# Heads 9, 17 and 25 by key layout in float32, their tiles one to two among those of the next two heads

## The chip, the cores and the metric

The kernel runs on one core of a Trainium2 chip. The metric is the device time of one execution in microseconds (us); several runs are given by their median. A profile of one execution shows what each engine did: PE (TensorE, matrix products), DVE (VectorE), ACT (ScalarE), POOL (GpSimd), SP (SyncE, which here issues most DMAs), and the 16 DMA engines.

## The reference

LSH attention on four batches of 8 heads, 768 positions, 64 wide, and then an MLP with spatial gating on the joined heads of each batch. Cut to what matters:

```
mask   = bucket(q) == bucket(k)                 # 6 hash bits, signs of q@proj, k@proj
scores = where(mask, q @ k.T / 8, -1e9)         # (4, 8, 768, 768)
scores = scores - max(scores, -1)
attn   = exp(scores) / (sum(exp(scores), -1) + 1e-9)
x      = (attn @ v) -> (4, 768, 512)
h      = relu(x @ w_in);  u, g = h[..., :512], h[..., 512:]
g      = (g - mean(g)) / sqrt(var(g) + 1e-6)
g      = einsum('ts,bsd->btd', w_spatial, g) + b_spatial
out    = (u * g) @ w_out
```

## The kernel before

Heads are numbered 0 to 31 (8 to a batch), pairs 0 to 15. A head has six **tiles** of 128 rows. A loop over g counts tiles: before, tile i of head n is worked on at g = 6n + i. In each step the loop names scores, value products, the preparation of later heads, the conversion of MLP weights and MLP units, and gives every piece a priority by `at(g + offset, k)`. A scheduler then puts the instructions of each engine in order by these priorities and by when it reckons them ready; each engine runs its list strictly in order, and so does each DMA queue.

**Query layout** (`scores`, head not in `KEYS`): the tile has 128 queries on the partitions and 768 keys along the row. Four fp16 matmuls (L291, L292; the hash mask is part of the product) fill a PSUM tile `sp`; DVE takes the row minimum of the scaled scores (L293, `jk`, result `nb`); ACT the exponential with that bias (L295, `ex`); ACT casts it to the fp16 high part (L298) and DVE or POOL subtracts to get the low part (L299), both into `pp`; a DMA transpose (L301) brings `pp` to `pt` with the keys on the partitions. Five tiles later (`LAG`) `weighted` multiplies `pt` with the fp16 high and low parts of v (`vp`): 18 matmuls (L314 to L316).

**Key layout** (`KEYS` = heads 1 to 7): the tile has 128 keys on the partitions. The row maximum must be known before: `row_max` makes the scores in query layout once more (two matmuls, L241), DVE takes their maximum (L243), and after the sixth tile the maxima are transposed on PE (L251) and sent by a small DMA into row 127 of the operand `ab` (L254). `scores_k` then needs four matmuls (L262, L263) and one exponential (L265, float32, into the same ring `pt` of `PTB` = 5 tiles); there is no cast, no subtraction and no transpose. Three tiles later (`LAGK`) `weighted_k` multiplies in float32 with `vf`, the values of a pair in float32 (L275). The row maxima of head n are named from `NT + LEAD` = 10 tiles before its first tile.

**Preparation.** `load_qk`, `hash_rows`, `split_qk` work by pairs; `build(n)` at g = 6(n - 2) issues the DMAs that fill one of four operands `ab` (L199 to L212): hash rows (`ab<-sg`, from ACT's queue for heads 8 and up) and the halves of q and k (`ab<-hl`, from SP's). `split_v` and `mean_v` prepare the values. `normalize` divides a finished head by its sum, `transpose_x` turns a pair for the MLP by DMA (`xt`).

**MLP.** When the last head of a batch is normalized, its 28 units (`vps`, `ups`, `sps`, `ops`) join a queue; a credit of 28/48 a step takes one out every 1.7 steps, so that the MLP of a batch runs on PE among the heads of the next one. That of batch 3 runs alone at the end.

PSUM has two tiles for scores (`sc`), two for value products (`pv`), two for the rest.

Of the kernel before, what the change touches and what calls it, by code (L numbers as in the profile page):

```python
# [19 lines left out]
P = 128  # L20
# [16 lines left out]
def lsh_attention_spatial_gating(  # L37
# [116 lines left out]
    def load_v(p):  # L154
        b, r = divmod(p, NPAIR)
        if has_queries(p):
            v32 = st["v32", p] = ld.tile([P, 2 * NT, D], F32, tag="v32", bufs=1, name=f"v32_{p}")
            LQ.dma_start(out=v32, in_=v[b, r])

    def load_vf(p):  # L160
        b, r = divmod(p, NPAIR)
        if has_keys(p):
            LQ.dma_start(out=vf[p % 2][:, :, 0:D], in_=v[b, r])

    def has_keys(p):
        return 2 * p in KEYS or 2 * p + 1 in KEYS

    def has_queries(p):
        return not (2 * p in KEYS and 2 * p + 1 in KEYS)

# [22 lines left out]
    def build(n):  # L193
        p, e = divmod(n, 2)
        hl, sg, t = st["hl", p], st["sg", p], ab[n % NAB]
        r = slice(D * e, D * e + D)
        q_s, q_h = (BQ_S[n >= NH], BQ_H[n >= NH])
        if n < 1:
            nc.sync.dma_start(out=t[0:D, 2:4], in_=hl[r, 1:3])  # L199
        for j in range(4):  # L200
            q_s.dma_start(
                out=t[D:NR, 3 - j // 2, (j % 2) * HS:(j % 2 + 1) * HS],
                in_=sg[32 * j + 16 * e:32 * j + 16 * e + 2 * NB, :])
        if n < 1:
            q_h.dma_start(out=t[0:D, 0:2], in_=hl[r, 0:2])
# [15 lines left out]
    def mean_v(p):  # L221
# [6 lines left out]
        nc.gpsimd.tensor_add(c, c, a[:, 4:6])  # L228
        mp = ps_m.tile([P, 512], F32, tag=MT, name=f"mp{p}")
        nc.tensor.matmul(mp[:, :P], lhsT=ones, rhs=c.rearrange("p e d -> p (e d)"), start=True, stop=True)  # L230
        fm = wk.tile([P, 2, D], F32, tag="fm", bufs=2, name=f"fm{p}")
        nc.scalar.activation(fm.rearrange("p e d -> p (e d)"), mp[:, :P], AF.Copy, scale=SX / S)
        st["fm", p] = fm

    def row_max(n, i):
        t = ab[n % NAB]
        if i == 0:
# [6 lines left out]
        if i == NT - 1:  # L244
            nb = st["nb", n] = wk.tile([P, NT], F32, tag="nb", bufs=3, name=f"nb{n}")
            mx = st.pop(("mx", n))
# [9 lines left out]
    def scores_k(n, i):  # L256
        t = ab[n % NAB]
        ps = ps_sc.tile([P, 2, 512], F32, tag="sc", name=f"sp{n}_{i}")[:, :, :HS]
# [9 lines left out]
    def weighted_k(n, i):  # L268
# [5 lines left out]
        for qi in range(NT):  # L274
            nc.tensor.matmul(acc[:, qi, :], lhsT=ex[:, qi * P:(qi + 1) * P], rhs=vf[p % 2][:, 2 * i + e, :],  # L275
                             start=(i == 0 and qi == 0), stop=(i == NT - 1 and qi == NT - 1))

    def scores(n, i):
        if n in KEYS:
            scores_k(n, i)  # L280
            return
        t = ab[n % NAB]
        if i == 0:
            st["nb", n] = wk.tile([P, NT], F32, tag="nb", bufs=3, name=f"nb{n}")
        nb = st["nb", n][:, i:i + 1]
# [32 lines left out]
    def normalize(n):  # L318
# [14 lines left out]
        nc.gpsimd.tensor_add(x, x, f)  # L333
        if e == 0:
            st["xs", p] = wk.tile([P, 2, NT, P], F16, tag="xs", bufs=2, name=f"xs{p}")
# [114 lines left out]
    PL_POOL = (2,)  # L450
    KEYS = {1, 2, 3, 4, 5, 6, 7}
    PL_POOL1 = (0,3)
# [32 lines left out]
    def at(g, k):  # L485
        tc.cur_priority = int(1000 * (g + 40) + k)

    at(-40, 0)
    nc.sync.dma_start(out=hc, in_=hconst)
# [11 lines left out]
    credit = 0.0  # L501
    wv = 0
    rml = [(NT * n + i - NT - LEAD, n, i) for n in sorted(KEYS) for i in range(NT)]
    for g in range(N * NT + LAG):
        n, i = divmod(g, NT)
        if n < N:
            at(g + G_S, 0)
            scores(n, i)
            r = n // 2
# [10 lines left out]
            while rml and rml[0][0] <= g:  # L520
                row_max(*rml.pop(0)[1:])
            at(g + G_P, 300)
            stack = ExitStack()
            if n not in KEYS:
                stack.enter_context(tc.issue_after(st["tr"]))
            if BQ_S[n + 2 >= NH] is nc.scalar or BQ_H[n + 2 >= NH] is nc.scalar:
                stack.enter_context(tc.issue_after(st["ex", n, i]))
            if i == BI and n + 2 < N:
                build(n + 2)
            if n % 2 == 0:  # L530
# [16 lines left out]
            stack.close()  # L547
        while wv < N * NT and wv + (LAGK if wv // NT in KEYS else LAG) <= g:
            m, j = divmod(wv, NT)
            wv += 1  # L550
            at(g + G_V, 200)
            weighted(m, j)
            if j == NT - 1:
                at(g + G_N, 250)
                normalize(m)
                if m % 2:
                    transpose_x(m // 2)
                    if m % NH == NH - 1:
                        queue += mlp_units(m // NH)
        at(g + G_W, 500)  # L560
# [53 lines left out]
```

## Time and profile before

| | |
|---|---|
| median of 3 runs | 738.57 us (736.13 to 741.49) |
| profiled execution, first to last instruction (span) | 741.7 us |
| mean granted PE clock | 0.937 |
| busy: PE, DVE, ACT, POOL | 631.5, 520.6, 434.8, 321.2 us |
| DMA | 120.95 MB, mean 163 GB/s |

The profile gives the span of the profiled execution, 0.4% above the median; no other time of that execution is shown. A row of a group is: line, engine, operation, output <- inputs, shape, count | busy us, mean ns of one | idle time of the engine before them and what ended it. A row of the timeline or of the chain begins with its start and its length in us; a row of waits gives the total, the number and the longest. Matmuls are pipelined, so a matmul's own duration is longer than the distance to the next one; distances are what count for PE.

### The profile page before, as it was taken

The page shows a single profiled execution, that of the slowest core. Times are in us where ns is not written, and L with a number is a line of the kernel's source. Part 1 is how long each engine was busy: PE and PEld are TensorE (multiplying, and loading weights), DVE is VectorE, ACT ScalarE, POOL GpSimd, SP SyncE. Part 2 cuts the span into 40 slices and gives each one's busy share as a digit, 9 for nine tenths or more (in the row PEclk, how much of TensorE's full clock was granted, in tenths as well). Part 3 has the DMA queues.
Part 4 walks back from the last instruction along what each step waited for, and adds up shares of the span by engine and source line. Part 5 has one row for each costly group of instructions (what it writes and reads, how often), then busy time and mean ns, then how long its engine had stood idle before and what let it go on. Part 6 is the DMA issues. An engine that isn't in the chain of part 4 may idle for free.

```text
span 741.7 us, 14927 instructions
## 1 busy us (share of the span) xinstructions
PE 631.5 (85%) x5759; PEld 400.4 (54%) x5759; DVE 520.6 (70%) x945; ACT 434.8 (59%) x668; POOL 321.2 (43%) x324
## 2 busy tenths in 40 slices
PE   1569898998988776997898899889898998999997
PEld 0237686776445444554544555556455565654553
DVE  4677795536799999567689798678698987755200
ACT  1344574346788676655676577667677776743221
POOL 5122443123458675264314565156235571451503
PEclk9768797999999989898999999999999999999999
DMA  9565554324999989996999799999999999860011
GB/s 235 149 123 155 133 148 102 99 55 97 224 237 197 215 207 187 213 178 138 234 202 199 138 210 213 211 211 212 206 210 181 194 175 213 182 136 15 1 42 43
DMA packets 290011, 120.95 MB, mean 163 GB/s; under 512 B 270740, under 2 KB 273812, under 8 KB 289940
## 3 DMA queue, kind: packets, MB, share of 16 engines
q1 hardware_dynamic: 287636, 119.11, 76.4%
q10 hardware_dynamic: 2304, 0.89, 0.5%
q8 instruction: 45, 0.74, 0.4%
q14 instruction: 26, 0.21, 0.1%
HBM read 28.33 MB, written 6.29 MB: 47 GB/s over the span
## 4 chain that ended last, share of the span: by engine, by line
PE 43%; DMA 21%; DVE 13%; issue 8%; ACT 6%; POOL 6%; SPq 3%; ACTq 0%; DVEq 0%; POOLq 0%
DMA pt<-pp 14%; PE pv L275 6%; PE vps L361 6%; PE ops L432 5%; PE sps L417 5%; PE ups L402 5%; DMA ab<-hl 4%; PE sp L291 3%; DVE jk L293 3%; PE sp L292 3%; DVE pp L299 2%; PE sp L262 2%; PE pv L314 2%; ACT ex L295 2%; PE sp L263 2%
## 5 line engine op out<-in xcount | busy, mean ns | idle before, releaser
L295 ACT ACTIVATE ex<-sp,nb 128x768 f32<-128x768 f32 x150 | 134.1, 897 | 54.8 <-DVE jk L293 48.9
L299 DVE TENSOR_TENSOR pp<-ex,pp 128x768 f16<-128x768 f32 x116 | 126.2, 1089 | 47.6 <-ACT pp L298 46.5
L293 DVE TENSOR_SCALAR_CACHE_REDUCE jk<-sp 128x768 bf16<-128x768 f32 x150 | 142.4, 949 | 24.1 <-PE sp L292 22.2
L298 ACT CAST pp<-ex 128x768 f16<-128x768 f32 x150 | 124.3, 829 | 50.0 <-DMA pt<-pp 43.9
L314 PE MATMUL pv<-vp,pt 128*128 128x65 f16 x900 | 108.2, 198 | 40.5 <-DMA pt<-pp 40.2
L291 PE MATMUL sp<-ab 128*128 128x384 f16 x300 | 103.2, 344 | 31.6 <-ACT ex L295 19.3
L314 PEld LDWEIGHTS <-pt 128*128 128x128 f16 x900 | 86.7, 101 | 67.2 <-DMA pt<-pp 53.4
L299 POOL TENSOR_TENSOR pp<-ex,pp 128x768 f16<-128x768 f32 x34 | 58.1, 1708 | 131.1 <-ACT pp L298 124.6
L315 PE MATMUL pv<-vp,pt 128*128 128x64 f16 x900 | 108.0, 197 | 0.0
L316 PE MATMUL pv<-vp,pt 128*128 128x65 f16 x900 | 107.8, 198 | 0.0
L292 PE MATMUL sp<-ab 127*128 127x384 f16 x300 | 103.9, 346 | 0.0
L417 PE MATMUL sps<-ws,vn 128*128 128x384 f16 x576 | 100.9, 329 | 1.5 <-DVE sg L180 1.0
L315 PEld LDWEIGHTS <-pt 128*128 128x128 f16 x900 | 87.0, 100 | 11.3 <-issue 1.3
L316 PEld LDWEIGHTS <-pt 128*128 128x128 f16 x900 | 86.9, 100 | 3.1 <-issue 0.5
L417 PEld LDWEIGHTS <-vn 128*128 128x128 f16 x576 | 55.3, 99 | 37.8 <-issue 3.9
L432 PE MATMUL ops<-wo,g 128*128 128x512 f16 x288 | 70.9, 391 | 1.5 <-ACT o L436 0.9
L275 PEld LDWEIGHTS pv<-vf,ex 128*128 128x128 f32 x504 | 68.5, 208 | 4.1 <-issue 1.6
L402 PE MATMUL ups<-xt,wi 128*128 128x384 f16 x384 | 69.1, 333 | 1.3 <-ACT u L405 0.9
L361 PE MATMUL vps<-wi,xt 128*128 128x512 f16 x288 | 68.0, 383 | 1.4 <-DMA xt<-xs 1.3
L275 PE MATMUL pv<-vf,ex 128*128 128x65 f32 x504 | 67.0, 286 | 0.0
L333 POOL TENSOR_TENSOR x<-x,xf 128x384 f32<-128x384 f32 x32 | 35.5, 1110 | 64.1 <-DVE x L332 64.1
L422 POOL TENSOR_TENSOR sy<-sy,u 128x384 f32<-128x384 f32 x32 | 36.6, 1145 | 49.3 <-DVE sy L421 49.2
(87 smaller groups left out, 1010.7 us busy)
## 6 DMA issues: line engine op xcount, KB each, us to landing
qk<-kq SPq DMA_DIRECT2D x16, 768.0 KB
ab<-hl SPq DMA_DIRECT2D x31, 384.0 KB
ab<-hl SPq DMA_DIRECT2D x34, 192.0 KB
out<-o SPq DMA_DIRECT2D x24, 256.0 KB
v<-v SPq DMA_DIRECT2D x13, 384.0 KB
raw<-w_in SPq DMA_DIRECT2D x16, 256.0 KB
pt<-pp SPq DMA_TRANSPOSE x150
raw<-w_sp SPq DMA_DIRECT2D x12, 192.0 KB
```

The lines of the kernel that those rows point to most:

```text
L275: nc.tensor.matmul(acc[:, qi, :], lhsT=ex[:, qi * P:(qi + 1) * P], rhs=vf[p % 2][:, 2 * i + e, :], start=(i == 0 and qi == 0), stop=(i == ...
L291: nc.tensor.matmul(ps[:, c], lhsT=t[:, 0, qs], rhs=t[:, 1, cs], start=True, stop=False)
L292: nc.tensor.matmul(ps[:, c], lhsT=t[0:P - 1, 3, qs], rhs=t[0:P - 1, 2, cs], start=False, stop=True)
L293: nc.vector.tensor_scalar(jk, ps, -ISQ, None, op0=ALU.mult, op1=ALU.min, accum_out=nb)
L295: st["ex", n, i] = nc.scalar.activation(ex, ps, AF.Exp, bias=nb, scale=ISQ).ins
L298: nc.scalar.copy(pp[:, 0], ex)
L299: (nc.gpsimd if i in (PL_POOL if n >= 2 * NH else PL_POOL1) else nc.vector).tensor_tensor(out=pp[:, 1], in0=ex, in1=pp[:, 0], op=ALU.subtract)
L314: nc.tensor.matmul(acc, lhsT=pt[:, c, :], rhs=vh, start=(i == 0 and c == 0), stop=False)
L315: nc.tensor.matmul(acc[:, 0:D], lhsT=pt[:, c, :], rhs=vl, start=False, stop=False)
L316: nc.tensor.matmul(acc, lhsT=pt[:, NT + c, :], rhs=vh, start=False, stop=(i == NT - 1 and c == NT - 1))
L361: nc.tensor.matmul(ps, lhsT=xt[c][:, gx, i * P:(i + 1) * P], rhs=wi[gw][:, c, F2:DF], start=(k == 0), stop=(k == 3 * NPAIR - 1))
L417: nc.tensor.matmul(ps[:, :HS], lhsT=vn[gv][:, c, d * P:(d + 1) * P], rhs=ws[gw][:, c, hs], start=(k == 0), stop=(k == 3 * NT - 1))
```

## The change

Heads 9, 17 and 25, one in each of batches 1 to 3, join the key layout (`KEYS` = `FIRST` | `SPREAD`). Their tiles no longer follow each other: each stands ahead of two tiles of the next two heads, so that heads 9, 10, 11 (and 17 to 19, 25 to 27) take 18 steps in which every third is a key tile. A table `order` gives the tile of each step and `place` its inverse; score steps, value products (`due`), row maxima (`rml`) and the choice of the operand `ab` (`slot`, `builds`) go by it. The builds themselves stay at g = 6(n - 2). The three heads read their values from a tile of their own, `vk` (float32, one head, loaded by `load_vk` four steps ahead of the head's first tile), while the rest of their pair still uses `vp`. The rings of `nb` and `fm` grow, and the sums of `mean_v` are kept in the `pf` tile, without a tile `vc`.

```diff
+    vk = const.tile([P, NT, D + 1], F32, name="vk")
+    nc.gpsimd.memset(vk[:, :, D:D + 1], 1.0)
...
+    def load_vk(n):
+        p, e = divmod(n, 2)
+        b, r = divmod(p, NPAIR)
+        LQ.dma_start(out=vk[:, :, 0:D], in_=v[b, r][:, e::2])
...
-        hl, sg, t = st["hl", p], st["sg", p], ab[n % NAB]
+        hl, sg, t = st["hl", p], st["sg", p], ab[slot[n]]
...
-        c = wk.tile([P, 2, D], F32, tag="vc", name=f"vc{p}")
-        nc.gpsimd.tensor_add(c, a[:, 0:2], a[:, 2:4])
+        c = a[:, 0:2]
+        nc.gpsimd.tensor_add(c, c, a[:, 2:4])
...
-            nc.tensor.matmul(acc[:, qi, :], lhsT=ex[:, qi * P:(qi + 1) * P], rhs=vf[p % 2][:, 2 * i + e, :],
+            nc.tensor.matmul(acc[:, qi, :], lhsT=ex[:, qi * P:(qi + 1) * P], rhs=vk[:, i] if n in SPREAD else vf[p % 2][:, 2 * i + e, :],
...
-    KEYS = {1, 2, 3, 4, 5, 6, 7}
+    FIRST = {1, 2, 3, 4, 5, 6, 7}
+    SPREAD = {8 * b + 1: (8 * b + 2, 8 * b + 3) for b in range(1, 4)}
+    KEYS = FIRST | set(SPREAD)
...
+    order, n = [], 0
+    while n < N:
+        if n in SPREAD:
+            others = [(m, i) for m in SPREAD[n] for i in range(NT)]
+            step = len(others) // NT
+            for i in range(NT):
+                order += [(n, i)] + others[step * i:step * i + step]
+            n += 1 + len(SPREAD[n])
+        else:
+            order += [(n, i) for i in range(NT)]
+            n += 1
+    place = {t: g for g, t in enumerate(order)}
...
+    for n in range(2, N):
+        k = min(range(NAB), key=lambda j: free[j])
+        slot[n] = k
+        builds.setdefault(max(NT * (n - 2) + BI, free[k]), []).append(n)
+        free[k] = place[n, NT - 1] + 1
+    rml = sorted((place[n, 0] - NT - LEAD + i, n, i) for n in KEYS for i in range(NT))
...
-            scores(n, i)
+            scores(*order[g])
...
+            for m in SPREAD:
+                if place[m, 0] - 4 == g:
+                    load_vk(m)
...
-        while wv < N * NT and wv + (LAGK if wv // NT in KEYS else LAG) <= g:
+        for m, j in due.get(g, ()):
```

More of the change, by code (lines that the diff above doesn't have):

```diff
@@ L555, in lsh_attention_spatial_gating @@
                 normalize(m)
[L556 removed]
+                half[m // 2] -= 1
+                if not half[m // 2]:
                     transpose_x(m // 2)
[L558 to L559 removed]
+                left[m // NH] -= 1
+                if not left[m // NH]:
+                    queue += mlp_units(m // NH)
         at(g + G_W, 500)
```

46 lines of the change are left out of this document (29 added, 17 removed).

## The prediction

> **What bounds the kernel now.** I read the page's slices first, then cut the span at the first exponential of each group of heads and asked for the engines' busy time in each stretch, then took the chain of waits and the rows of single instructions. The slices:
>
> ```profile
> PE   1569898998988776997898899889898998999997
> DVE  4677795536799999567689798678698987755200
> PEclk9768797999999989898999999999999999999999
> DMA  9565554324999989996999799999999999860011
> ```
>
> A slice is 18.5 us. Slices 4 to 9 are batch 0 with its key heads: PE full, the DMA engines half idle. From slice 10 to 34, where the 24 query heads of batches 1 to 3 run, DMA and PE are both near full. The last four are the MLP of batch 3 alone. The change touches the middle. The stretches below begin at heads 8, 9, 12, 16, 17, 20, 24, 25 and 28; the cuts come from the exponentials of L295, six to a head, in program order.
>
> ```profile
> 175.00:189.50 14.50, 9.96 (x82) 6.14 (x80) 11.26 (x20) 10.39 (x15) 8.30 (x8) 0.88 0.72 135
> 189.50:251.40 61.90, 54.69 (x562) 32.30 (x561) 57.51 (x101) 50.93 (x86) 39.03 (x34) 0.97 1.05 221
> 251.40:347.00 95.60, 73.57 (x724) 45.74 (x724) 76.34 (x131) 59.81 (x95) 51.64 (x48) 0.90 0.95 191
> 347.00:364.00 17.00, 16.33 (x164) 9.41 (x161) 11.09 (x17) 10.59 (x15) 5.22 (x5) 0.88 0.84 181
> 364.00:427.20 63.20, 52.30 (x547) 30.91 (x548) 52.42 (x103) 42.52 (x63) 25.77 (x23) 0.97 0.95 187
> 427.20:498.10 70.90, 61.39 (x673) 38.94 (x672) 56.27 (x99) 48.81 (x70) 32.86 (x33) 0.98 1.04 212
> 498.10:517.80 19.70, 19.70 (x219) 12.93 (x218) 17.75 (x31) 13.61 (x19) 12.38 (x11) 1.00 0.97 210
> 517.80:576.00 58.20, 52.85 (x525) 31.15 (x524) 46.77 (x97) 41.17 (x64) 23.46 (x23) 0.94 0.99 197
> ```
>
> The columns are length, then PE, weight loads, DVE, ACT and POOL busy, granted clock, DMA share, GB/s. The three stretches that the change rewrites are those of 61.90, 63.20 and 58.20 us: PE is idle in them for 7.2, 10.9 and 5.35 us, and the DMA share is 0.95 to 1.05. In front of two of them, at heads 16 and 24, PE is busy for 16.33 of 17.00 and 19.70 of 19.70 us. So two resources stand close together, and the change takes from one and gives to the other. What PE waits for, and what the chain holds:
>
> ```profile
> PE pv L314 <- DMA pt<-pp: 34.5, 29, 4.0
> PE sp L291 <- ACT ex L295: 18.9, 15, 5.1
> PE 43%; DMA 21%; DVE 13%; issue 8%; ACT 6%; POOL 6%; SPq 3%; ACTq 0%; DVEq 0%; POOLq 0%
> DMA pt<-pp 14%; PE pv L275 6%; PE vps L361 6%; PE ops L432 5%; PE sps L417 5%; PE ups L402 5%; DMA ab<-hl 4%; PE sp L291 3%; DVE jk L293 3%; PE sp L292 3%; DVE pp L299 2%; PE sp L262 2%; PE pv L314 2%; ACT ex L295 2%; PE sp L263 2%
> ```
>
> From head 8 on, the longest wait of PE is for the transposes of the probabilities, 34.5 us in 29 times, and they hold 14% of the chain.
>
> **What leaves.** Each of the 18 tiles of heads 9, 17 and 25 loses its transpose (132 are left of 150). A transpose moves 128x1536 two-byte values, 0.393 MB; at the 212 GB/s of the stretch with DMA share 1.04 that is 1.86 us, 33.4 us for 18. Each key head gets its values by a load of 0.197 MB, 0.93 us at the same rate, 2.8 us for three. The DMA engines lose some 30.6 us of work. DVE, ACT and POOL lose work too:
>
> ```profile
> L293 DVE TENSOR_SCALAR_CACHE_REDUCE jk<-sp 128x768 bf16<-128x768 f32 x150 | 142.4, 949 | 24.1 <-PE sp L292 22.2
> L299 DVE TENSOR_TENSOR pp<-ex,pp 128x768 f16<-128x768 f32 x116 | 126.2, 1089 | 47.6 <-ACT pp L298 46.5
> L298 ACT CAST pp<-ex 128x768 f16<-128x768 f32 x150 | 124.3, 829 | 50.0 <-DMA pt<-pp 43.9
> L243 DVE TENSOR_REDUCE mx<-mp 128x1 f32<-128x768 f32 x42 | 39.8, 952 | 23.3 <-PE mp L241 23.2
> ```
>
> A key tile has a row maximum of 952 ns for the 949 ns minimum, no cast (829 ns on ACT) and no subtraction (1089 ns on DVE or longer on POOL). Six tiles free at most 6.5 us of DVE and 5.0 us of ACT in a stretch. In the first, where DVE is busy for 57.51 of 61.90 us, that keeps it from being the bound; in the others DVE has 11 us free already. I give it no term of its own.
>
> **What PE gets.** The pitch of its instructions, from the timeline and the chain:
>
> ```profile
> 524.03 0.33 PE L291 MATMUL sp<-ab 128*128 128x384 f16 x1
> 524.69 0.19 PE L314 MATMUL pv<-vp,pt 128*128 128x65 f16 x1
> 525.20 0.19 PE L316 MATMUL pv<-vp,pt 128*128 128x65 f16 x1
> 100.91 0.48 PE L241 MATMUL mp<-ab 127*128 127x384 f16 x2
> 101.24 0.33 PE L262 MATMUL sp<-ab 128*128 128x384 f16 x1
> 105.21 1.28 PE pv L275 x12
> ```
>
> A query tile's four score matmuls take 0.66 us (524.03 to 524.69), its 18 value matmuls 0.54 us (17 pitches of 0.03 us to 525.20, and one more). A key tile's value product is twelve PE instructions in 1.28 us. Its scores cost the same as a query tile's, and its row maximum two matmuls more, 0.33 us. So each key tile adds 0.74 us of PE in its stretch, **4.4 us a head**, and **2.0 us a head** for the row maxima some ten tiles earlier.
>
> The Trainium skill, "FP8 and Floating Point Precision", section "TensorE Precision Notes", gives true FP32 four passes through the array. By that rule six products of 65 columns at four times the 0.03 us pitch would be an estimated 0.72 us, and the three heads would cost PE 10 us less. The row of 1.28 us disagrees, and the sum goes by the row.
>
> **Where the instructions go.** On SP, at the head that follows head 16, the order before and the order after (pt16_5 is the transpose of head 16's last tile, v32 and ab are loads):
>
> ```order
> L301 DMA_TRANSPOSE pt16_5_4225<-pp16_5_4222 128x12x128
> L344 DMA_TRANSPOSE xt7_4209<-xs7_3943 128x12x128
> L301 DMA_TRANSPOSE pt17_0_4289<-pp17_0_4286 128x12x128
> L211 DMA ab3_85<-hl9_3878 64x2x1536
> L212 DMA ab3_85<-hl9_3878 64x1536
> L301 DMA_TRANSPOSE pt17_1_4327<-pp17_1_4324 128x12x128
> ```
>
> ```order
> L308 DMA_TRANSPOSE pt16_5_4173<-pp16_5_4170 128x12x128
> L308 DMA_TRANSPOSE pt18_0_4267<-pp18_0_4264 128x12x128
> L160 DMA v32_10_4269<-v 128x768
> L308 DMA_TRANSPOSE pt18_1_4319<-pp18_1_4316 128x12x128
> L218 DMA ab0_82<-hl10_4355 64x2x1536
> L219 DMA ab0_82<-hl10_4355 64x1536
> L308 DMA_TRANSPOSE pt18_2_4434<-pp18_2_4431 128x12x128
> ```
>
> Head 17's transposes are gone and head 18's stand in their place. On PE, three tiles before the end of head 15, where head 17's row maximum (mp17) now enters; before:
>
> ```order
> L316 MATMUL pv14_3659<-vp1_95,pt14_3_3541 128x65
> L291 LDWEIGHTS ab3_85
> L291 MATMUL sp15_3_3865<-ab3_85 128x384
> L292 LDWEIGHTS ab3_85
> L292 MATMUL sp15_3_3865<-ab3_85 128x384
> ```
>
> ```order
> L424 MATMUL sps0_3_1_3758<-ws0_106,vn0_0_1685 128x384
> L248 LDWEIGHTS ab2_84
> L248 MATMUL mp17_0_3727<-ab2_84 128x384
> L298 LDWEIGHTS ab3_85
> L298 MATMUL sp15_3_3783<-ab3_85 128x384
> ```
>
> After the change the scores of tile 15_3 stand behind a matmul that reads ab2, which the build of head 17 fills two tiles earlier; what stays queued behind a late ab2 is every score and value matmul of heads 14 and 15.
>
> **The sum, against the profiled span of 741.7 us.**
>
> *Start.* The first load of vk stands in SP's queue ahead of head 0's operands.
>
> ```profile
> 2.13 2.61 SPq L163 DMA_DIRECT2D vf<-v  x2
> 4.78 2.92 SPq L126 DMA_DIRECT2D bt<-b_sp  x1
> 7.74 0.54 SPq L199 DMA_DIRECT2D ab<-hl  x1
> 8.77 0.50 SPq L205 DMA_DIRECT2D ab<-hl  x1
> 14.47 6.02 DMA ab<-sg
> ```
>
> A vf load takes 1.3 us to issue; vk has half its pieces, so 0.65 to 1.3 us, of which SP's pause from 8.28 to 8.77 hides 0.5. The 0.197 MB also go ahead of the ab<-sg that lands 6.02 us after its issue: up to 0.9 us. Range 0.2 to 1.7, taken +0.9.
>
> *Row maxima.* Heads 16 and 24 have PE full, and so has the end of batch 0: +6.0 (0 if they fall into waits).
>
> *The stretches.* If PE alone then sets them, they take 54.69 + 4.4 = 59.1, 52.30 + 4.4 = 56.7 and 52.85 + 4.4 = 57.25 us in place of 61.90, 63.20 and 58.20: -2.8, -6.5 and -0.95, together **-10.3**. The DMA work left in them is under this: share times length, 65.0, 60.0 and 57.6 us, less six transposes (11.2 us), is 53.8, 48.8 and 46.4 us. The other end, if PE keeps every wait, is +13.2.
>
> *Behind the stretches.* They end with a shorter DMA queue than before.
>
> ```profile
> 358.98 6.17 DMA pt<-pp
> 654.16 3.38 DMA pt<-pp
> ```
>
> A transpose in a full queue needs 6.17 us to land, the last one, with nothing ahead, 3.38. The difference is the backlog that a stretch inherits, 2.8 us; it can be saved once behind each stretch. Range 0 to -8.4, taken -7.2, near the full difference since the DMA share of the next stretch is 1.04 in batch 2 and the saving is spent at once.
>
> *The new wait.* mp17 waits for its ab.
>
> ```profile
> 74.92 4.03 DMA ab<-hl
> 289.54 6.07 DMA ab<-hl
> ```
>
> Such a load lands 4.03 us after its issue in batch 0 and 6.07 us in a full queue. The row maximum comes two tiles after the build, 7.0 us at 63.20 us for 18 tiles, but the build's issue itself stands behind a transpose that waits for its data. Nothing if the two tiles cover it, up to 5 us a head otherwise; taken +1 a head, +3.0.
>
> I cost at nothing: the memset of vk (POOL, before its first use), the larger rings of nb and fm, and the mean's partial sums, now in the pf tile until PE's mean matmul has read them; the next user of pf comes some four tiles later. Uncovered, that is a wait such as
>
> ```profile
> PE mp L230 <- POOL vc L228: 6.7, 4, 3.7
> ```
>
> Sum: 0.9 + 6.0 - 10.3 - 7.2 + 3.0 = **-7.6 us**, 741.7 to 734.1. The runs' median, 738.57, is 0.9958 of the profiled span: **731.0 us**, 1.0% faster. One per cent is about what a measurement of this kernel can tell from no change.
>
> **Rivals.** *DMA was the bound and PE's extra hides in its waits*: the whole 30.6 us come off, 711.1, or 708 on the scale of the median. For it: DMA share near 1 for 450 us. Against: PE is idle for only 23 us in the three stretches, and full in front of two; half of it (720) is as far as I believe it.
>
> *PE becomes the bound and nothing is left*: a quarter of the waits stays (23.45 / 4 = 5.9 us), so -4.4 in the stretches, -3 behind them, and +6.0, +0.9 and +3.0 as before: +2.5, about 741. For it: the lengths that PE allows, 59.1, 56.7 and 57.25, are a gain in one stretch of three only.
>
> *Slower: the row maximum stalls PE and the clock drops.* mp waits for the build of its own head, behind a full DMA queue, for 5 us, and PE then runs at a lower clock:
>
> ```profile
> 80.00:90.00 10.00, 8.03 (x35) 6.87 (x35) 7.17 (x14) 5.08 (x11) 6.06 (x7) 0.57 0.44 119
> 83.21 2.66 PE L275 MATMUL pv<-vf,ex 128*128 128x65 f32 x12
> ```
>
> Twelve instructions took 2.66 us here against 1.28, at clock 0.57: 8.03 us of PE at that clock lose some 3.4. Price 8.4 a head, 25 in all in place of 3.0: 756, or 753 on the median's scale. It decides from the point at which ab lands more than two tiles after its issue. The Trainium skill, "TensorE: Matmul & The Clock Gate", section "What's actually happening", has PE fall to half clock after an idle window of about 3.4 us; the row of 0.57 agrees, and by that rule a stall under that length costs only itself.
>
> That the change does not do what it says is excluded by the order: 18 transposes are gone and the key tiles stand one to two.
>
> **How the numbers follow.** Forecast (722 to 735) 0.45; DMA bound (700 to 722) 0.15; nothing left (735 to 743) 0.24; stall (743 to 760) 0.16. Of the forecast two thirds lie under 731.2, 1% below the median: faster 0.30 + 0.15 = 0.45; within 1% 0.15 + 0.24 = 0.39; slower 0.16. The range takes in half of each outer rival: 714 to 750.
>
> **What would show it.** 132 transposes; the exponentials of heads 9 to 12, 17 to 20 and 25 to 28 some 59, 57 and 57 us apart with PE over 95% busy and DMA share under 0.9; heads 15 and 16, and 23 and 24, together some 2 us longer where mp enters; no PE wait on ab over 2 us at L248. I am wrong if PE waits there, if the DMA share stays near 1 in the stretches, or if the gaps between the stretches change more than the stretches do.

## The result and the profile after

The changed kernel takes **770.34 us**, median of 4 runs (766.32 to 772.93), against 738.33 of the kernel before on the same chip (736.13 to 741.49): ratio **1.0438** [1.0387, 1.0489]. The prediction of 731.0 us was wrong in sign. The profiled execution has a span of 771.0 us against 741.7, so there are 29.3 us to place. The profiles of two experiments below (contiguous; matmuls alone) come from disturbed executions; their ratios are used and no row of them.

The same slices as before, now 19.3 us each:

```profile
PE   1569898996998958887799979897899989899997
DVE  3666786637566787676767897768478766754200
PEclk9956799999999979998899989999899999999999
DMA  9673546217965699996977599996967699961011
```

The DMA row has what was meant: 6 and 7 where three in a row stood at 9. The PE row did not become fuller for it. To see where the time went I cut both spans at the first exponentials of the same heads. The kernel before, first: head 8, heads 9 to 11, 15, 16, 17 to 19, 23, 24, 25 to 27 (columns as in the prediction: length, PE, weight loads, DVE, ACT, POOL, clock, DMA share, GB/s).

```profile
174.90:189.70 14.80, 10.26 (x83) 6.37 (x82) 11.29 (x20) 10.69 (x15) 8.30 (x8) 0.88 0.73 137
189.70:253.00 63.30, 55.01 (x565) 32.47 (x564) 59.09 (x103) 52.33 (x89) 39.21 (x35) 0.97 1.07 223
326.40:349.40 23.00, 17.82 (x172) 10.91 (x171) 16.26 (x27) 13.60 (x19) 12.50 (x12) 0.89 0.73 148
349.40:368.20 18.80, 16.31 (x186) 9.79 (x185) 12.18 (x22) 12.26 (x16) 5.08 (x6) 0.96 1.03 236
368.20:432.50 64.30, 53.69 (x551) 31.58 (x549) 53.95 (x103) 42.76 (x65) 26.39 (x24) 0.97 0.95 180
490.20:508.80 18.60, 18.60 (x196) 11.94 (x194) 16.71 (x30) 12.84 (x18) 8.68 (x8) 0.98 1.08 213
508.80:530.40 21.60, 19.49 (x203) 11.98 (x201) 14.67 (x26) 13.55 (x22) 12.24 (x12) 0.96 1.09 229
530.40:587.10 56.70, 52.83 (x551) 31.70 (x550) 50.79 (x101) 42.21 (x64) 24.53 (x21) 0.96 0.97 192
```

And the changed kernel, the same eight pieces:

```profile
178.00:201.20 23.20, 16.49 (x137) 8.79 (x135) 16.01 (x28) 16.32 (x24) 11.78 (x12) 0.93 0.88 177
201.20:269.70 68.50, 62.36 (x546) 39.73 (x545) 48.07 (x92) 45.72 (x83) 38.82 (x37) 0.95 0.72 156
333.60:365.20 31.60, 27.05 (x260) 15.96 (x259) 21.80 (x33) 14.23 (x20) 13.74 (x13) 0.88 0.85 160
365.20:387.80 22.60, 16.20 (x145) 9.21 (x145) 16.18 (x28) 13.65 (x19) 7.89 (x8) 0.82 0.93 186
387.80:442.70 54.90, 53.72 (x513) 35.52 (x511) 42.70 (x81) 36.42 (x56) 22.09 (x20) 1.00 0.65 137
501.20:531.70 30.50, 26.21 (x287) 16.31 (x286) 21.89 (x37) 15.12 (x21) 14.36 (x14) 1.00 0.91 157
531.70:555.20 23.50, 17.73 (x137) 9.99 (x137) 15.52 (x28) 14.09 (x19) 6.43 (x8) 0.85 1.07 215
555.20:609.90 54.70, 53.91 (x529) 36.07 (x528) 42.71 (x83) 36.50 (x57) 21.86 (x20) 1.00 0.73 144
```

The last two stretches do what was forecast: PE busy 53.72 of 54.90 and 53.91 of 54.70 us at clock 1.00, DMA share 0.65 and 0.73, 9.4 and 2.0 us shorter. The loss is **where the row maxima are made**: head 15 grows by 8.6 us and head 23 by 11.9, and the heads behind them, 16 and 24, by 3.8 and 1.9. Head 8 grows too, from 14.8 to 23.2 us, but that is not the row maxima's doing: it takes 22.5 us without them (first experiment below). In head 23 PE gets 287 instructions in place of 196 between the first exponentials of heads 23 and 24, and 18.60 of 18.60 us busy becomes 26.21 of 30.50. The timeline of ACT in that head shows the scores thinning out; the kernel after, first exponential to last:

```profile
501.17 0.92 ACT L302 ACTIVATE ex<-sp,nb 128x768 f32<-128x768 f32 x1
...
506.65 0.90 ACT L302 ACTIVATE ex<-sp,nb 128x768 f32<-128x768 f32 x1
...
508.32 0.90 ACT L302 ACTIVATE ex<-sp,nb 128x768 f32<-128x768 f32 x1
...
517.25 0.90 ACT L302 ACTIVATE ex<-sp,nb 128x768 f32<-128x768 f32 x1 [1.38 <-DVE jk L300]
...
523.51 0.90 ACT L302 ACTIVATE ex<-sp,nb 128x768 f32<-128x768 f32 x1 [2.44 <-DVE jk L300]
...
528.32 0.90 ACT L302 ACTIVATE ex<-sp,nb 128x768 f32<-128x768 f32 x1 [0.38 <-DVE jk L300]
```

Between 508.32 and 523.51 two exponentials start in 15 us, where a tile takes about 3 in a stretch. PE was not idle meanwhile; it did value products and MLP units that stand ahead of the scores. With late scores the transposes are issued late, and the next head seems to pay for it: PE is idle for 6.4 of 22.6 us in head 16 and 5.8 of 23.5 in head 24 (2.5 and 2.1 before).

What PE waits for in the whole changed kernel:

```profile
PE pv L321 <- DMA pt<-pp: 46.4, 36, 3.4
PE sp L298 <- DMA ab<-hl: 10.9, 1, 10.9
PE sp L298 <- DVE mx L250: 9.2, 8, 1.7
PE sp L298 <- ACT ex L302: 7.9, 9, 2.2
...
PE mp L248 <- DVE mx L250: 5.2, 4, 3.1
PE mp L248 <- DMA ab<-hl: 4.8, 2, 3.1
```

There are 18 transposes fewer, and the wait for transposes is longer, 46.4 us in place of 40.2. It did not grow everywhere. In two stretches, those of heads 17 to 19 and 25 to 27, it nearly vanished (1.2 and 0.4 us, 5.2 and 3.5 before), as was meant. It grew most in heads 15, 16, 23 and 24, from 2.5 to 10.7 us together, and from head 28 on, from 2.2 to 8.1. In those four heads no transpose on the chain was slow, and these are the two longest of six:

```profile
536.20 5.49 DMA pt<-pp
...
544.43 5.61 DMA pt<-pp
```

The other four took 3.8 to 5.0 us. The chain of the kernel before has 6.17 and 7.13 us there, in heads 16 and 24. So in these heads, as far as the chain shows, PE waits for transposes that started late rather than for slow ones. From head 28 on that does not hold: one on the chain took 7.93 us. The new wait that I feared, a row maximum for its operand, is not it: of the 4.8 us, 1.8 lie in head 23 and the rest in batch 0.

**One sum over everything.** Up to the first exponential of head 7 the change does nothing but the late start (24.9 to 26.1 us). From there to the end, before:

```profile
160.60:741.70 581.10, 510.64 (x4923) 311.98 (x4922) 417.98 (x752) 363.62 (x552) 268.85 (x247) 0.96 0.84 171
```

and after:

```profile
162.40:771.00 608.60, 535.74 (x4854) 330.72 (x4853) 403.31 (x726) 352.07 (x534) 256.74 (x246) 0.95 0.77 152
```

PE is busy for 25.1 us more. The forecast had 19.3 (13.3 for the value products, 6.0 for the row maxima); the lower clock, 0.95 for 0.96, would by proportion make some 5 of it, an estimate from two rounded means. But **PE's idle time did not shrink**: 70.5 us before, 72.9 after. The forecast needed it to shrink by some 28. The experiments ask why.

### The profile page after: what moved, and what is told of

Same layout as the page of the kernel before. It is cut to its first block, busy times and chain, and to the rows that moved or that the text cites. A ratio compares the mean times of both kernels' runs of the same rounds, so it can differ in the third digit from the quotient of the medians.

```text
span 771.0 us, 14637 instructions
## 1 busy us (share of the span) xinstructions
PE 656.7 (85%) x5690; PEld 419.1 (54%) x5690; DVE 502.6 (65%) x919; ACT 422.4 (55%) x650; POOL 305.1 (40%) x324
## 4 chain that ended last, share of the span: by engine, by line
PE 44%; DMA 23%; DVE 14%; ACT 7%; issue 6%; POOL 3%; SPq 2%; ACTq 0%; DVEq 0%; POOLq 0%
DMA pt<-pp 15%; PE sps L424 7%; PE ups L409 7%; PE pv L282 6%; PE ops L439 5%; DMA ab<-hl 4%; PE vps L368 3%; DVE jk L300 3%; PE sp L298 3%; PE sp L299 3%; DVE pp L306 2%; PE pv L321 2%; PE sp L269 2%; PE sp L270 2%; ACT pp L305 2%
## 5 line engine op out<-in xcount | busy, mean ns | idle before, releaser
L302 ACT ACTIVATE ex<-sp,nb 128x768 f32<-128x768 f32 x132 | 118.5, 899 | 91.8 <-DVE jk L300 88.9
L300 DVE TENSOR_SCALAR_CACHE_REDUCE jk<-sp 128x768 bf16<-128x768 f32 x132 | 125.4, 950 | 54.3 <-PE sp L299 53.8
L321 PE MATMUL pv<-vp,pt 128*128 128x65 f16 x792 | 95.6, 198 | 47.2 <-DMA pt<-pp 46.4
L305 ACT CAST pp<-ex 128x768 f16<-128x768 f32 x132 | 109.5, 830 | 37.3 <-DMA pt<-pp 24.9
L306 DVE TENSOR_TENSOR pp<-ex,pp 128x768 f16<-128x768 f32 x102 | 107.2, 1053 | 24.9 <-ACT pp L305 23.4
L298 PE MATMUL sp<-ab 128*128 128x384 f16 x264 | 92.7, 351 | 28.1 <-DMA ab<-hl 10.9
L321 PEld LDWEIGHTS <-pt 128*128 128x128 f16 x792 | 77.0, 102 | 72.0 <-DMA pt<-pp 63.5
L322 PE MATMUL pv<-vp,pt 128*128 128x64 f16 x792 | 95.6, 197 | 0.0
L323 PE MATMUL pv<-vp,pt 128*128 128x65 f16 x792 | 95.5, 199 | 0.0
L322 PEld LDWEIGHTS <-pt 128*128 128x128 f16 x792 | 77.2, 101 | 8.0 <-issue 1.8
L323 PEld LDWEIGHTS <-pt 128*128 128x128 f16 x792 | 77.3, 101 | 3.5 <-issue 1.4
L250 DVE TENSOR_REDUCE mx<-mp 128x1 f32<-128x768 f32 x60 | 57.0, 953 | 25.2 <-PE mp L248 25.0
L272 ACT ACTIVATE ex<-sp 128x768 f32<-128x768 f32 x60 | 48.4, 806 | 42.4 <-PE sp L270 39.0
```

Source lines behind the costliest of these rows:

```text
L298: nc.tensor.matmul(ps[:, c], lhsT=t[:, 0, qs], rhs=t[:, 1, cs], start=True, stop=False)
L300: nc.vector.tensor_scalar(jk, ps, -ISQ, None, op0=ALU.mult, op1=ALU.min, accum_out=nb)
L302: st["ex", n, i] = nc.scalar.activation(ex, ps, AF.Exp, bias=nb, scale=ISQ).ins
L305: nc.scalar.copy(pp[:, 0], ex)
L306: (nc.gpsimd if i in (PL_POOL if n >= 2 * NH else PL_POOL1) else nc.vector).tensor_tensor(out=pp[:, 1], in0=ex, in1=pp[:, 0], op=ALU.subtract)
L321: nc.tensor.matmul(acc, lhsT=pt[:, c, :], rhs=vh, start=(i == 0 and c == 0), stop=False)
```

## The experiments

The column "from head 7" is this stretch of the profiled execution, split into PE busy and idle; it leaves out the first heads, which no edit reaches (a section below says why that matters). The last four columns of a row are of one execution, and executions of one kernel differ: the profiled one took 738.9 us for a median of 745.28 (reductions alone) and 764.8 for one of 759.12 (row maxima in MLP's PSUM). So a few us between two rows decide nothing by themselves. Each ratio is to the kernel before on the same chip.

| kernel | median us | ratio [95%] | from head 7 | PE busy | PE idle | clock |
|---|---|---|---|---|---|---|
| before | 738.33 | | 581.1 | 510.6 | 70.5 | 0.96 |
| after | 770.34 | 1.0438 [1.0387, 1.0489] | 608.6 | 535.7 | 72.9 | 0.95 |
| order only | 747.99 | 1.0183 [1.0132, 1.0234] | 591.2 | 512.6 | 78.6 | 0.96 |
| no row maxima | 734.91 | 1.0012 [0.9969, 1.0056] | 580.5 | 519.4 | 61.1 | 0.97 |
| contiguous | 770.87 | 1.0463 [1.0398, 1.0527] | | | | |
| contiguous, no row maxima | 755.33 | 1.0259 [1.0192, 1.0326] | 591.3 | 521.2 | 70.1 | 0.97 |
| row maxima four steps later | 766.38 | 1.0435 [1.0378, 1.0491] | 607.0 | 536.1 | 70.9 | 0.94 |
| row maxima in MLP's PSUM | 759.12 | 1.0272 [1.0183, 1.0360] | 605.7 | 537.2 | 68.5 | 0.95 |
| matmuls alone | 756.38 | 1.0238 [1.0140, 1.0336] | | | | |
| reductions alone | 745.28 | 1.0078 [1.0031, 1.0125] | 581.7 | 515.8 | 65.9 | 0.97 |
| tail alone | 748.64 | 1.0138 [1.0063, 1.0213] | 585.2 | 522.4 | 62.8 | 0.96 |
| lead kept | 751.37 | 1.0213 [1.0160, 1.0266] | 597.8 | 528.7 | 69.1 | 0.97 |
| lead kept, four steps later | 762.79 | 1.0299 [1.0235, 1.0364] | 598.5 | 528.0 | 70.5 | 0.96 |
| lead kept, MLP held too | 749.69 | 1.0154 [1.0077, 1.0231] | 592.8 | 530.0 | 62.8 | 0.96 |
| lead kept, matmuls alone | 747.64 | 1.0155 [1.0095, 1.0214] | 590.9 | 527.7 | 63.2 | 0.96 |
| before + row maxima | 761.66 | 1.0357 [1.0302, 1.0412] | 600.1 | 524.2 | 75.9 | 0.95 |
| the same, lead kept | 752.89 | 1.0160 [1.0097, 1.0222] | 591.6 | 516.4 | 75.2 | 0.97 |
| no row maxima, two-byte products | 745.40 | 1.0129 [1.0076, 1.0183] | 583.6 | 511.6 | 72.0 | 0.94 |

### Which part of the change costs: four edits

**No row maxima** for heads 9, 17 and 25 (the shift comes from an old row of `ab` and a tile of zeros):

```diff
-    rml = sorted((place[n, 0] - NT - LEAD + i, n, i) for n in KEYS for i in range(NT))
+    rml = sorted((place[n, 0] - NT - LEAD + i, n, i) for n in FIRST for i in range(NT))
```

> The changed kernel without the row maxima of heads 9, 17 and 25 (their shift comes from an old row and a zero; the rest is as changed). Theory A, the row maxima in front of the stretches hold back the score tiles and cost far more than their 6 us of PE: 738 to 745 us, and the exponentials of heads 15 to 16 and 23 to 24 as far apart as before (23 and 19 us, not 32 and 31). Theory B, the stretches are bound by PE's extra work: 6 us less than the change, 762 to 766. Theory C, the one-to-two order itself costs: 760 or more.

Measured 734.91, level with before. The 18 row maxima, whose matmuls are 6 us of PE, carry the whole loss: 31 us between the ratios (0.0426 of 738), 28.1 from head 7. Its row, beside those above:

```profile
152.70:733.20 580.50, 519.35 (x4815) 323.94 (x4814) 379.64 (x702) 350.20 (x534) 253.74 (x246) 0.97 0.81 159
```

Without them PE's idle time does fall, to 61.1 us, 9.4 less than before, while PE is busy for 8.8 us more; the two cancel.

**Contiguous**: all tiles of the key head first, then those of the next two.

```diff
-            for i in range(NT):
-                order += [(n, i)] + others[step * i:step * i + step]
+            order += [(n, i) for i in range(NT)] + others
```

> The same three heads by key layout, but their tiles in a row, no spreading. Theory A: about as slow as the change, 762 to 775, since the row maxima stand at the same steps. Theory B (PE bound in the stretches): slower than the change, 775 to 785, since 18 key tiles in a row need 2.3 us of PE each beside the MLP. Theory C (the order costs): faster than the change, 740 to 755.

770.87, the same as spread. That looked as if spreading did nothing, until the row maxima were taken out of both (below).

**Order only**: `KEYS = FIRST` and no load of `vk`, so that heads 9, 17 and 25 keep the query layout and their transposes, in the one-to-two order; their last tiles multiply the values of a later pair.

> Only the one-to-two order, all heads of batches 1 to 3 in query layout, no row maxima. Theory A and theory B: the time of before, 735 to 745. Theory C: 755 to 775.

747.99, 1.0183, between the ranges expected: **the order without key tiles costs 10.1 us** from head 7, 8.1 of it PE idle. Its waits name the cause:

```profile
PE pv L321 <- DMA pt<-pp: 37.1, 40, 3.4
PE sp L298 <- ACT ex L302: 33.0, 25, 3.0
```

and the kernel before, over the whole span:

```profile
PE pv L314 <- DMA pt<-pp: 40.2, 32, 4.0
PE sp L291 <- ACT ex L295: 19.3, 16, 5.1
```

Scores wait for a free tile, that is for an exponential, 33.0 us in place of 19.3. I had given the order no cost. With key tiles in it the order is a gain, though; the experiment contiguous, no row maxima, below, shows that.

**Row maxima four steps later**, at the end of the head before:

```diff
-    rml = sorted((place[n, 0] - NT - LEAD + i, n, i) for n in KEYS for i in range(NT))
+    rml = sorted((place[n, 0] - NT - (0 if n in SPREAD else LEAD) + i, n, i) for n in KEYS for i in range(NT))
```

> The row maxima of the three heads four steps later, beside heads 8, 16 and 24, where the MLP leaves PE free. Theory A with PE's load as the reason: 745 to 755, the loss at heads 15 and 23 gone. Theory A with the hold on the score tiles as the reason (they share the two PSUM tiles): the loss moves to heads 16 and 24 and stays, 762 to 775. Theory B: no difference, 768 to 773.

766.38, no change of the ratio. Heads 15 and 23 are back at 19.3 us each in its profile, but heads 16 to 19 and 24 to 27 grow to 83.7 and 88.9 (77.5 and 78.2 after). The loss moves with the row maxima; their place is not what makes it.

### What of a row maximum costs

A row maximum is two matmuls into a score tile, DVE's reduction, and after six of them a tail: rounding, PE's transpose, a copy and a small DMA. In the next runs one part is moved or others are left out. The tail stays in all of them:

**In MLP's PSUM tiles**, so that no score tile is held:

```diff
+                pm = ps_m.tile([P, 512], F32, tag=MT, name=f"mp{n}_{i}_{c}")
+                nc.tensor.matmul(pm[:, :HS], ...)
+                nc.vector.reduce_max(st["mh", n][:, i, c:c + 1], pm[:, :HS], axis=AX.X)
```

> The row maxima of the three heads stay where they are, but their matmuls write the two PSUM tiles of the MLP (one half each, two reductions of 384) and not the two of the scores. Theory S, the loss comes from sharing the two score tiles: 735 to 748 us. Theory D, the reductions on DVE cost it: 765 to 775, as they are 36 now. Theory T, the transposed maxima and their DMA cost it: 765 to 775.

759.12, between the ranges expected. By the ratio a part of the loss goes, but from head 7 only 2.9 us (605.7 for 608.6). Heads 15 and 23 are short again (18.9 and 18.0 us), and heads 16 to 19 and 24 to 27 take 86.5 and 90.1. So sharing the two score tiles decides in which heads the loss falls; it is not the whole price. What holds heads 16 and 24 up here stays open; PE waits for transposes there for 8.2 and 6.7 us.

**Matmuls alone** (with the tail): DVE's reduction left out for the three heads, `mx` is a tile of zeros.

```diff
+        if n not in SPREAD:
             nc.vector.reduce_max(st["mx", n][:, i:i + 1], ps, axis=AX.XY)
```

> The matmuls of the row maxima stay, in the score tiles, but nothing reads them: no reduction on DVE (the maxima are zero). Theory S: still slow, 755 to 770, a little less since a score tile is held for PE's time only. Theory D: 735 to 745. Theory T: 765 to 773.

756.38, 1.0238: about half of the loss remains (0.0226 of 0.0426).

**Reductions alone** (with the tail): no matmuls; DVE reduces a tile that lies in SBUF (`reduce_max(..., bt)`).

> No matmuls for the row maxima; DVE reduces a tile of the same 128x768 float32 that lies in SBUF, at the same steps (the maxima are meaningless). Theory S: 735 to 747. Theory D: 755 to 770. Theory T: 765 to 773.

745.28, 1.0078. That is 0.0066 over the kernel without row maxima, and 1.2 us from head 7: little.

**Tail alone**: neither matmuls nor reductions.

> No matmuls and no reductions; only the end of the row maxima stays: rounding, transpose on PE, copy and the DMA into the operand (of zeros). Theories S and D: 733 to 742. Theory T: 755 to 770.

748.64, 1.0138, between the ranges expected; from head 7 it is 4.7 us over the kernel without row maxima. The tail with the reductions came out cheaper than the tail without them, by 3.5 us, so both figures are no better than that. Either way the reductions cost nothing that can be seen while no matmul fills a score tile for them.

### The order on PE

The order of PE's list shows what the matmuls do to it. Count, at each score tile, how many tiles have been scored and not yet begun in their value product; call it the **lead**. A product that comes too soon behind its scores must wait for the chain of exponential, cast, subtraction and transpose. Steps 92 to 99 (heads 15 and 16) and 141 to 145 (heads 23 and 24):

```
                       steps 92 to 99      steps 141 to 145
before                 4 5 4 5 5 4 4 4     4 4 5 4 5
after                  4 3 3 2 1 2 3 3     2 2 2 2 2
no row maxima          4 4 5 5 5 4 4 4     4 4 4 4 4
in MLP's PSUM          4 5 4 5 4 4 4 3     3 4 4 5 5
lead kept              4 4 4 4 4 4 4 4     4 4 4 4 4
```

The scheduler puts the row maxima where it reckons a score tile free. It seems that scores then find a free tile later, and that it fills PE with value products and MLP units in the meantime. In the stretches the lead is 3 to 4 after, and 4 to 5 before; a key tile's shorter lag (`LAGK`) takes part in that, since it is about 4 without row maxima too.

**Lead kept**: around heads 8, 16 and 24 a value product may not go ahead of the scores of the step before.

```diff
+    HOLD = {g for b in range(1, 4) for g in range(48 * b - 4, 48 * b + 8)}
...
+            with ExitStack() as es:
+                if g in HOLD and g < N * NT:
+                    es.enter_context(tc.issue_after(st["sc", *order[g - 1]]))
+                weighted(m, j)
```

> The changed kernel, row maxima in the score tiles and all, but around them (steps 44 to 55, 92 to 103, 140 to 151) the value product of a tile is ordered on PE behind the scores of the tile one step back, so that scores keep a lead of four tiles over value products (two in batch 0). Theory O, the loss is the order on PE, where value products and MLP units pass the scores: 735 to 752 us, segments 15 to 16 and 23 to 24 back to some 22 us. Theory P, the loss is that a row maximum holds one of two score tiles on the chip, whatever the order: 762 to 775, PE waits in front of scores.

751.37: 1.0438 becomes 1.0213, half of the loss, with the same instructions. From head 7 10.8 us come back, 7.0 of them as PE busy time, at clock 0.97 in place of 0.95, and 3.8 as idle time:

```profile
151.20:749.00 597.80, 528.69 (x4855) 328.18 (x4853) 404.42 (x726) 352.36 (x534) 258.22 (x246) 0.97 0.78 155
```

One part of the expectation failed: heads 15 and 23 are not back at 22 us. They take 28.3 and 30.6 us, for 31.6 and 30.5 after; heads 16 and 24 come down by 2.5 and 2.1. So the order of the value products is not what keeps heads 15 and 23 long. And in the run with the row maxima in MLP's PSUM the lead is 3 to 5 without any hold, and the loss from head 7 is nearly whole: a kept lead alone does not remove it.

**Before + row maxima**: the kernel before, with row maxima of heads 9, 17 and 25 that nobody uses; **the same, lead kept**, has the hold as well.

```diff
-    rml = [(NT * n + i - NT - LEAD, n, i) for n in sorted(KEYS) for i in range(NT)]
+    rml = sorted((NT * n + i - NT - LEAD, n, i) for n in sorted(KEYS | {9, 17, 25}) for i in range(NT))
```

> The kernel before, with the row maxima of heads 9, 17 and 25 added at the same ten steps ahead, in the score tiles, and left unused; no layout change, no spreading. Theories O and P: the loss comes with the row maxima alone, 758 to 775 us. Theory I, it needs the spread key heads: 738 to 750 (6 us of PE, 17 of DVE, partly hidden).

> The kernel before with the unused row maxima (762) and with the lead of scores kept around them. Theory O: 738 to 748. Theory P: 752 to 764. Half and half as in the changed kernel: 746 to 754.

1.0357, and 1.0160 with the hold. From head 7 that is 19.0 us over the kernel before, and 10.5 with the hold. Most of the loss, and its coming down by about half, are there without new key heads, without the new order and without `vk`; both kernels leave out the tail as well. It belongs to the row maxima.

**Lead kept, row maxima four steps later** (both edits, `HOLD` from 48b - 2 to 48b + 11), and **lead kept, MLP held too** (the units of a step in `HOLD` not ahead of its scores):

> As the run with the lead kept, and the row maxima four steps later, away from the hash and split of the next pair on DVE (split_qk stands at step 93, the row maxima at 92 to 97). Theory O+D, what is left at heads 15 and 23 is the row maximum waiting behind split_qk on DVE while it holds a score tile: 737 to 747. Theory P, each row maximum costs by holding one of two score tiles wherever it stands: 749 to 758.

> As the run with the lead kept, and around the row maxima the MLP units too are ordered behind the scores of their own step. If what is left at heads 15 and 23 is MLP units that pass the scores (59 matmuls stood between two score tiles there): 737 to 745. If it is the hold on the score tiles (P) or the wait behind split_qk (O+D): 748 to 754.

762.79: with the hold, later row maxima are no better than at the old place, against what I expected (the ratio is worse, the stretch from head 7 the same, 598.5 against 597.8). 749.69 with MLP held: 5.0 us from head 7, though the ratio (1.0154 against 1.0213) can't tell it from nothing.

**Lead kept, matmuls alone**, for what remains:

> Left out: DVE's reductions of the row maxima of heads 9, 17 and 25 (their tile is filled with zeros); their matmuls, rounding, transpose, copy and DMA are there, and around heads 8, 16 and 24 a value product is held until the scores of the step before are issued, as in the kernel with the lead kept (751.37 us, 1.0213). Theory D (what is left there after the order is mended is DVE's reduction, for which the two tiles of scores wait): 740 to 747 us, ratio 1.004 to 1.011. Theory P (it is PE's matmuls and their hold on the tiles of scores): 749 to 755 us, ratio 1.015 to 1.023. Between the two: both share it.

747.64, and 590.9 from head 7: 6.9 under the kernel with the lead kept, 10.4 over that without row maxima. Its median lies between the two ranges expected and its ratio at the edge of the second, so both seem to share the rest; the ratio alone (1.0155 against 1.0213) can't tell it from the lead kept. The 10.4 are near the tail's 4.7 and the matmuls' 6.0 together. The four heads around the row maxima give the same picture with less around it. Heads 15, 16, 23 and 24 together take 82.0 us before, 108.2 after, 100.4 with the lead kept, 93.6 with the reductions gone as well, 88.8 with the tail alone and 83.4 without row maxima. That the reductions matter, the waits show too: with the lead kept PE waits 3.7 and 2.8 us for them in heads 15 and 23. Where DVE's part comes in, the timeline of the changed kernel shows at the end of head 15:

```profile
345.39 0.95 DVE L300 TENSOR_SCALAR_CACHE_REDUCE jk<-sp 128x768 bf16<-128x768 f32 x1
...
346.27 0.95 DVE L250 TENSOR_REDUCE mx<-mp 128x1 f32<-128x768 f32 x1
...
348.69 1.46 DVE L196 SCALAR_TENSOR_TENSOR hl<-qk,hl 128x768 f16<-128x768 f32 x1 [0.44 <-ACT hl L195]
350.07 2.39 DVE L197 SCALAR_TENSOR_TENSOR hl<-qk,hl 128x768 f16<-128x768 f32 x1
...
353.57 0.94 DVE L300 TENSOR_SCALAR_CACHE_REDUCE jk<-sp 128x768 bf16<-128x768 f32 x1
...
354.45 0.95 DVE L250 TENSOR_REDUCE mx<-mp 128x1 f32<-128x768 f32 x1
```

The split of q and k, 3.85 us, stands in DVE's list between two minima; both score tiles, one of them a row maximum's, wait behind it and are read from 353.57 and 354.45. A reduction that costs little without matmuls (581.7) probably costs here because the scores need the tile that waits for it.

### Why the relief is not seen

**Contiguous, no row maxima**: both edits together.

> Three key heads, tiles in a row, without their row maxima (shift from an old row and a zero). If spreading brings the relief of the DMA queue: 743 to 755, slower than the spread kernel without row maxima (735). If it brings nothing: 730 to 741. If the row maxima are the loss here as well (O, P): far under the 771 with them either way.

755.33 against 734.91 spread. Spreading is worth 10.8 us from head 7 (591.3 to 580.5), 9.0 of it PE idle time: contiguous key tiles leave that at 70.1 us, as before; spread it is 61.1. The ratios differ by more, 0.0247 or 18 us, but 7.8 us of that lie before head 7 in the profiles, where no edit reaches.

This run also says that the two halves of the change belong together. Against the kernel before, from head 7, the order alone costs 10.1 us and key tiles in the old order cost 10.2; both together cost nothing (-0.6). Over the whole kernel PE's wait for an exponential ahead of a query tile's scores is 19.3 us before, 33.0 with the order alone, 24.2 with key tiles alone and 9.0 with both.

**No row maxima, two-byte products** for the three heads:

```diff
-        ex = wk.tile([P, S], F32, tag="pt", bufs=PTB, name=f"ex{n}_{i}")
+        ex = wk.tile([P, S], F16 if n in SPREAD else F32, tag="pt", bufs=PTB, name=f"ex{n}_{i}")
...
-            ... rhs=vk[:, i] if n in SPREAD else vf[p % 2][:, 2 * i + e, :],
+            ... rhs=vp[p % 2][:, 2 * i + e, D:2 * D + 1] if n in SPREAD else vf[p % 2][:, 2 * i + e, :],
```

> Left out: the row maxima of heads 9, 17 and 25, and the float32 of their value products: their exponentials are written in two bytes, and the six products of a tile read them and the two-byte high part of the pair's values. All else, the order of the tiles too, is that of the kernel without the row maxima (734.91 us, 1.0012). A key tile's value product then is six instructions in place of twelve; at the 0.03 us pitch of a two-byte product some 0.2 us in place of 1.28, 19 us of PE less in the 18 tiles. Theory P (the float32 products eat what the missing transposes give back, PE is the bound of the stretches): at least half of the 19 us come off, 715 to 726 us, ratio 0.970 to 0.987, and the three stretches together shrink by 8 us or more. Rival W (the stretches wait for transposes and tiles of scores in the new order, and PE's work fills waits that were there): 730 to 736 us, ratio 0.993 to 1.001.

```profile
162.80:746.40 583.60, 511.60 (x4707) 307.15 (x4706) 387.55 (x702) 349.08 (x534) 258.66 (x246) 0.94 0.80 158
```

745.40, slower than with float32 and above the range of either theory. Theory P does not hold: PE had 7.8 us less busy time at a lower clock, and 10.9 us more of idle. From head 7 the two kernels are 3.1 us apart; the rest, 10.1 us, lies before head 7, which the edit does not touch. So taking PE's float32 price away brings no gain. The lower clock, 0.94 for 0.97, came with it and blurs the comparison.

## Why the prediction was wrong, step by step

- **Start**, +0.9: the first exponential moved from 24.9 to 26.1 us, +1.2. Right.
- **Stretches**, -2.8, -6.5, -0.95: my cuts were up to three tiles early (I put head 25 at 517.8 us; it starts at 530.4), so the rows above are the ones to compare: +5.2, -9.4, -2.0, together -6.2 for -10.3. In the last two the mechanism is the one forecast, PE full. The first holds more of batch 0's MLP: 62.36 us of PE, where 55.01 + 4.4 were reckoned.
- **Row maxima, +6.0, and their new wait, +3.0**: the step that failed first. Measured 28.1 us from head 7 in place of 9.0. By experiments, in succession: 10.8 come back when value products are held behind the scores, 6.9 more when DVE's reductions are left out, and 10.4 are matmuls and tail, of which the matmuls' 6.0 are the only part that I had. On PE the 28.1 are 16.3 us busy and 11.8 idle; beyond the matmuls' 6.0 the busy part is about what the lower clock makes (0.95 for 0.97, by proportion an estimated 10 us). I priced an instruction by its duration. What it costs here is more: it holds a score tile until DVE has read it, it delays the scores behind it, and the clock falls with the waits. Which of these weighs most, the runs do not settle.
- **The relief, -10.3 in the stretches and -7.2 behind them**: the second step that failed. Together -17.5; measured without row maxima, key layout and order together, -0.6 from head 7 (581.1 to 580.5). So from head 7 the forecast was +9.0 - 17.5 = -8.5, and +28.1 - 0.6 = +27.5 was measured; 1.2 of start and 0.6 between make the 29.3.
- **What I never priced: how order and layout act on each other.** The order costs 10.1 us without key tiles, and saves 10.8 with them.
- **Behind the stretches**, -7.2: heads 12 to 14, 20 to 22 and 28 to 30 changed by -9.5, +0.8 and +6.4 us. The first is PE work that moved into the stretch ahead (57.6 us of PE before, 49.5 after), and no saving of a backlog is seen in the others: 6.17 and 3.38 us, from which I took it, are two transposes on the chain, and the DMA share behind the stretches is still 1.03 to 1.12. Why heads 28 to 30 take longer in nearly all the reordered kernels stays open.
- **PE does wait less**: without row maxima its idle time is 61.1 us in place of 70.5. But PE is busy for 8.8 us more, where 13.3 were reckoned for the dearer products. For -17.5 its idle time would have had to fall by some 31 us; it fell by 9.4.
- **The slower rival** had the place right and the mechanism only in part. It wanted a wait for the operand; L248 waited 1.8 us for it in head 23. Its second half, the lower clock, is there: 0.82 and 0.85 in heads 16 and 24, where PE idles for transposes, and from head 7 a mean of 0.95, which is 0.97 with the lead kept. The Trainium skill, "TensorE: Matmul & The Clock Gate", section "What's actually happening", lets PE fall to half clock after an idle window of about 3.4 us. The half clock is in these traces, but shorter waits were enough: in head 24 it followed a wait of 2.37 us (rows in the last section). So the prediction was wrong that the row of 0.57 bears out the page's rule in full, and that a stall under that length costs only itself; in the kernel before the longest wait ahead of that row was 2.07 us.
- **DMA as the bound**, the fast rival: out for the changed kernel. In two stretches the DMA share is 0.65 and 0.73, and PE, not a transfer, sets their length.
- **The signs named** were the right ones to watch: 132 transposes, PE over 95% in two of the three stretches, DMA share 0.65 to 0.73, and "the gaps between the stretches change more than the stretches do", which is what happened.

No version here beats the kernel before.

## What to carry to other kernels

An instruction that borrows a tile from a ring of two can cost several times its duration; here 28 us were lost where 6 us of matmuls were reckoned. Look in the order for how far the producers run ahead of the consumers, and who else must read the tile, not only at the added busy time. A wait for a transfer can be a late start rather than a slow transfer; in heads 15, 16, 23 and 24 the transposes on the chain took 3.8 to 5.6 us in place of 6.17 and 7.13, and the wait for them grew. And test a change's parts separately and together: the gain of spreading (10.8 us from head 7) could not be seen while the row maxima hid it, and order and key layout, each a loss alone, cancel together.

## What was not expected of the hardware

The part of the span ahead of head 7 has the same 816 PE instructions in these two kernels, and took 136.3 us after, 126.9 without row maxima. After:

```profile
26.10:162.40 136.30, 115.68 (x816) 87.13 (x816) 88.74 (x179) 65.36 (x113) 40.11 (x59) 0.85 0.51 124
```

Without row maxima:

```profile
25.80:152.70 126.90, 107.53 (x816) 81.08 (x816) 89.41 (x179) 65.52 (x113) 40.08 (x59) 0.95 0.56 133
```

Over the profiles of all kernels it ranges from 125.0 to 137.2 us and the granted clock there from 0.81 to 0.99, though no edit reaches these heads. Ten microseconds is 1.4% of the time, as much as several of the effects measured here, so a single execution is best compared from the place where the kernels differ. Why it varies stays open.

The clock falls to half after shorter waits than I thought. In head 24 of the changed kernel, and in batch 0 of the kernel before:

```profile
544.10:547.40 3.30, 0.93 (x20) 0.49 (x17) 1.25 (x3) 0.16 (x1) 2.62 (x5) 1.00 1.07 118
547.50:554.30 6.80, 5.91 (x46) 3.72 (x43) 4.15 (x6) 4.74 (x8) 1.16 (x2) 0.50 1.18 234
```

```profile
78.00:81.30 3.30, 1.90 (x16) 1.61 (x15) 1.53 (x3) 1.87 (x3) 1.59 (x3) 1.00 1.04 269
81.40:91.60 10.20, 9.63 (x39) 7.54 (x39) 6.72 (x14) 4.28 (x10) 5.56 (x7) 0.50 0.38 100
```

The waits ahead of the two drops, after and before:

```profile
547.21 0.20 PE L321 MATMUL pv<-vp,pt 128*128 128x65 f16 x1 [2.37 <-DMA pt<-pp]
```

```profile
81.97 0.48 PE L262 MATMUL sp<-ab 128*128 128x384 f16 x1 [2.07 <-ACT ex L265]
```

Ahead of the first drop PE was busy for 0.93 of 3.30 us, ahead of the second for 1.90 of 3.30. Each time the clock stayed at 0.50 for 6.8 and 10.2 us though PE was busy again.
